# Gated linear attention into a cosine-gated MLP on one core: the first pair through the MLP as one unit of 256 tokens, pair 4 turned by DMA, 52 zero products for 54, and a new order of all steps

## The chip, the cores and the metric

The kernel runs on 1 core of one Trainium2 chip. The metric is the device time of one execution in microseconds (us). Three runs of the kernel before gave 182.62, 182.84 and 184.4 us; the median is 182.84 us.

## The reference

Two stages follow each other. The first is a gated linear attention over 4 batches, 8 heads, 768 positions and a head width of 48; the second is an MLP (the kernel's names call it MoE, though it has one expert) over the 3072 tokens that come out, with 384 inputs and 2048 hidden features.

```python
f = 1.0 / (1.0 + np.exp(-f_logit))                 # (4, 8, 768, 48)
for t in range(S):
    state = f[:, :, t, :, None] * state + np.einsum('bhd,bhe->bhde', k[:, :, t], v[:, :, t])
    y[:, :, t] = np.einsum('bhd,bhde->bhe', q[:, :, t], state)
x = y.transpose(0, 2, 1, 3).reshape(B * S, H * D)  # (3072, 384)
h = x @ w_in                                       # (3072, 2048)
g = h * np.cos(h)
out = g @ w_out                                    # (3072, 384)
```

All inputs and the output are float32 in DRAM; products are made in bf16.

## The kernel before

**Tiling.** The tokens are cut into 12 pairs of 256 tokens (two blocks of 128), three pairs to a batch. Within a pair the attention is done block-wise with matrix products, and a state (`sz`) is carried from block to block and from pair to pair. The MLP is done in units: `UNITS` cuts the 3072 tokens into two units of 128 tokens (both halves of pair 0) and then eleven of 256.

**Steps.** `describe` makes some 950 named steps with what each reads and writes. In a name the number is the pair (for the MLP the unit). Those that matter below are, in the order in which a pair passes through them:

- `f`, `k`, `q`, `v`: the loads, 384 KB each (192 KB for the halves `.0` and `.1` in pairs 0 and 1). `w0.i`, `w1.i`: the loads of the four quarters of `w_in` and of `w_out`, 768 KB each, into slots of the buffer `g`; `wc0.i`, `wc1.i`: their casts to bf16.
- `ex`, `ln`, `fx`, `fy` (ScalarE): exponentials and logarithms of the gate. `ad` (GpSimd) and `cum` (TensorE): their sums along the tokens. `eb`, `ei` (ScalarE): the decays. `qa`, `ka`, `qm`, `km` (GpSimd or VectorE): q and k with the decays in them.
- `tq`, `tk`: q and k turned. For pairs outside `TURN_QK` these are eight TensorE transposes for each half of the heads (line 435), with a copy `qkt` out of PSUM; for pairs in `TURN_QK` it is one DMA transpose for each half (line 424), issued from the SP queue.
- `sc` (line 456): scores, 8 products of 48x128 for each half where TensorE turned, 16 of 48x64 where the DMA did. `am` (VectorE): the mask. `ps` (line 479), `st`, `sz`: the state. `y`, `yi` (line 531): the pair's attention output, `xe`: its copy to `x`.
- `h` (line 579): x times `w_in`, 6 products for each step of a 256-token unit, 12 for each step of a 128-token unit. `co` (ScalarE, line 584): cosine. `g` (VectorE, line 561): h times its cosine. `o` (line 595): g times `w_out`, four products a step. `ot`, `out`: the copy and the store of 128 tokens.
- `zf`: a product of a zero tile with itself, 128x512, whose result nobody reads (line 264). `ZEROS` says how many there are.

**What sets the order.** `ORDER` is one long string. Each word names a step, the engine that does it (T TensorE, S ScalarE, V VectorE, G GpSimd, Y the SP queue) and, behind that, the buffer slots or PSUM banks that it takes. `emit` makes the instructions in the order of the words; each engine and each queue does its own instructions strictly in that order, and waits in front of an instruction until what it needs is there. SP issues nearly all loads, stores and DMA transposes from one queue.

```python
    for word in ORDER.split():
        name, how = word.split(":")
        plan.append((G.steps[name], LETTER[how[0]], [int(x) for x in how[1:].split(",") if x]))
    ...
        s.fn(e)
```

Of the kernel before, what the change touches and what calls it, by code (L numbers as in the profile page):

```python
# [15 lines left out]
B, H, S, D = 4, 8, 768, 48  # L16
# [11 lines left out]
TURN_QK = range(5, 12)  # L28
UNITS = [128, 128] + [256] * 11
# [3 lines left out]
ZEROS = 54  # L33
# [3 lines left out]
zvt.2:V zsp.1:V zsp.0:G zsz.3:V f0.1:Y0 f0.0:S zqk.0:G k0.0:Y0 ex0.1:S ex0.0:S k0.1:Y ln0.1:S1  # L37
zf0:T0 zf1:T0 zf2:T0 zf3:T0 zf4:T0 zf5:T0 zf6:T0 zf7:T0 zf8:T0 zf9:T0 cum0.1:T0 ln0.0:S cum0.0:T1
fx0.0:S ei0.1:S0 fx0.1:S ei0.0:S ka0.0:V f1.1:Y1 km0.0:G0 f1.0:Y ex1.1:S ka0.1:V zf10:T2 zf11:T2
zf12:T2 zf13:T2 zf14:T2 zf15:T2 zf16:T2 zf17:T2 tk0.0:T2 eb0.1:S0 ex1.0:S ln1.1:S1 ln1.0:S fx1.0:S  # L40
q0.1:Y0 q0.0:Y v0:Y0 fx1.1:S eb0.0:S qa0.1:V zqk.1:V qm0.1:V vb0:S0 f3:Y2 k1.1:Y1 km0.1:V qa0.0:V
zf18:T3 cum1.1:T3 zf19:T4 zf20:T4 zf21:T4 tq0.1:T0 cum1.0:T1 qm0.0:G zsz.2:G eb1.0:S1 vt0.3:S2
k1.0:Y ei1.0:S0 ex3:S zf22:T4 zf23:T4 zf24:T4 zf25:T4 zf26:T4 ps0.1:T4,5 ps0.0:T tk0.1:T v1:Y1 f2:Y0
qkt0.1:V0 eb1.1:S ln3:S0 ei1.1:S ka1.0:G q1.0:Y0 tq0.0:T ka1.1:G km1.1:G0 zvt.1:G vt0.0:S ad3:G1
vt0.1:G q1.1:Y vb1:S1 qkt0.0:V1 vt0.2:G zsz.1:G ex2:S w0.1:Y0 w0.0:Y1 k3:Y0 q3:Y1 w0.3:Y2 ln2:S1
vt1.2:S1 fy3:S zf27:T6 zf28:T6 zf29:T6 zf30:T6 zf31:T6 zf32:T6 sc0.0:T0 sz0.01:V2 sz0.00:V w0.2:Y3
ad2:G0 vt1.0:G km1.0:V vt1.3:G wc0.1:G am0.0:V0 zf33:T6 zf34:T6 yi0:T4 sc0.1:T2 am0.1:V1 st0.11:V
sz0.11:V3 wc0.0:G k2:Y1 zf35:T6 zf36:T6 zf37:T6 zf38:T6 ps1.1:T6,7 tk1.0:T0 ps1.0:T zf39:T1 zf40:T1
zf41:T1 cum3:T1 fy2:S ei3:S0 fx3:S ka3:G eb3:S2 vt1.1:S fx2:S km3.0:G1 qa3:G qm3.0:G km3.1:G qm3.1:G
w1.0:Y0 qa1.0:V st0.10:V qa1.1:V qm1.0:V wc0.2:G ka2:G q2:Y2 tk1.1:T2 zf42:T3 zf43:T3 y0:T3 tq1.0:T  # L50
xe0.1:S0 sz0.10:V st1.00:V st1.01:V qm1.1:V v2:Y1 zf44:T5 zf45:T5 zf46:T5 zf47:T5 zf48:T5 tq1.1:T
cum2:T1 sz1.00:V1 qkt1.0:V0 eb2:S0 xe0.0:S ei2:S1 qkt1.1:V1 km2.0:G0 km2.1:G zf49:T5 sc1.0:T4
sz1.01:V zf50:T0 zf51:T0 sc1.1:T2 h0.01:T0 st1.11:V sz1.11:V2 am1.1:V0 wc1.0:G qa2:G zf52:T6 zf53:T6
h0.00:T co0.0:S0 qm2.1:G am1.0:V1 h1.01:T2 h1.00:T co1.0:S1 y1:T6,4 yi1:T g0.0:V1 xe1.1:V1 st1.10:V
qm2.0:G vb2:G1 sz1.10:V g1.0:V4 w1.2:Y3 xe1.0:S tk3.0:T5 h2.01:T0 tq3.0:T w1.3:Y0 qkt3.0:V0 v3:Y0
f4:Y0 h2.10:T6 h2.00:T sc3.0:T4 tq3.1:T2 tk3.1:T h2.11:T wc1.2:G wc1.3:G vt2.1:G1 wc0.3:S vb3:G0
co2.0:S1 am3.0:V0 g2.0:V2 h2.20:T4 h2.21:T h0.11:T0 co2.1:S0 qkt3.1:S1 co2.2:S1 sc3.1:T2 w1.1:Y3
g2.1:V am3.1:V1 g2.2:V h0.10:T h1.11:T6 h1.10:T h2.30:T2 tk2.1:T4 tk2.0:T5 co0.1:S0 co1.1:S2 g0.1:V
g1.1:V h2.31:T o2.0:T0 co2.3:S0 tq2.1:T vt3.2:G2 vt3.1:G tq2.0:T o0.0:T1 o3.0:T6 o1.0:T7 qkt2.0:S2
vt2.0:S g2.3:V qkt2.1:V3 sc2.0:T2 ex4:S o3.2:T o0.2:T am2.0:V2 ln4:S1 ps2.0:T4 sc2.1:T2 vt2.3:G  # L60
ps2.1:T am2.1:V3 st2.01:V st2.00:V sz2.01:V1 sz2.00:V wc1.1:S f5:Y2 ex5:S ln5:S0 o1.2:T o2.3:T
o3.3:T o0.3:T o2.2:T q4:Y2 ps3.0:T4,5 ps3.1:T zsz.0:G vt2.2:G ad4:G0 yi2:T2,3 y2:T vt3.3:G sz3.01:V0
sz3.00:V o1.3:T cum4:T4 v4:Y0 vt3.0:G ad5:G0 fy4:S eb4:S0 st3.11:V fx4:S k4:Y1 fy5:S qa4:G qm4.0:G1
fx5:S ei4:S1 o0.1:T o2.1:T o3.1:T xe2.0:V1 st3.10:V sz3.10:V1 qm4.1:G sz3.11:V xe2.1:V ot2:V0
h3.00:T2 o1.1:T cum5:T0 ei5:S0 eb5:S2 k5:Y0 h3.01:T ot0:V1 vb4:G0 ka4:G y3:T4,5 yi3:T q5:Y1 h3.10:T0
h3.11:T co3.0:S0 xe3.0:V0 xe3.1:V ot1:V2 ot3:V3 co3.1:S2 g3.0:V4 h3.21:T4 h3.20:T co3.2:S1 h4.21:T6
h4.20:T g3.1:V ka5:G km4.0:G co4.2:S0 km4.1:G vt4.1:G2 qa5:G h4.11:T2 h4.10:T g3.2:V co4.1:S2
h4.31:T0 k6:Y2 qm5.1:G0 h4.30:T vt4.0:G vt4.2:G km5.1:G f6:Y1 v5:Y0 v6:Y1 f7:Y0 tq4.0:T4 tq4.1:T5
out3:Y tk4.0:T tk4.1:T co4.3:S1 g4.2:V2 h3.31:T6 h3.30:T qkt4.1:S0 qkt4.0:V1 g4.1:V o5.1:T4 co3.3:S0
o5.2:T o5.0:T o4.1:T5 g4.3:V g3.3:V ps4.1:T0,1 ps4.0:T st4.01:V st4.00:V sc4.1:T2 sc4.0:T6 am4.1:V0  # L70
am4.0:V1 sz4.00:V0 sz4.01:V qm5.0:G vt4.3:G st4.10:V tq5.1:Y2 sz4.10:V2 o5.3:T o4.2:T km5.0:G o4.0:T
o4.3:T ex6:S ln6:S0 vb6:G0 ad6:G0 ex7:S cum6:T2 y4:T3,6 tq5.0:Y3 yi4:T ot5:S3 st4.11:V sz4.11:V
vb5:G1 fx6:S ln7:S1 ei6:S0 eb6:S1 xe4.1:S1 o6.2:T4 out5:Y ad7:G0 ka6:G km6.0:G1 km6.1:G vt5.0:G2
vt5.1:G ps5.0:T2 ps5.1:T xe4.0:S st5.01:V sc5.0:T6 am5.0:V0 out0:Y k7:Y0 q6:Y1 q7:Y2 fy6:S fx7:S
f9:Y2 sc5.1:T0 cum7:T3 o6.3:T o6.1:T vt5.3:G h4.01:T6 h4.00:T st5.00:V am5.1:V1 sz5.01:V0 vt6.3:G1
qa6:G eb7:S0 ot4:S1 ka7:G ei7:S1 ps6.1:T3,5 ps6.0:T sz6.01:V1 sz5.00:V sz6.00:V v7:Y0 co4.0:S0
qm6.0:G h5.00:T0 h5.01:T co5.0:S1 vt5.2:S g4.0:V st6.11:V fy7:S h5.31:T2 h5.30:T o6.0:T y5:T6,7
yi5:T g5.0:V4 co5.3:S0 ot6:S3 tq6.0:Y0 xe5.1:S0 xe5.0:S f8:Y1 km7.0:G0 qa7:G km7.1:G qm7.1:G qm7.0:G
qm6.1:G h5.20:T0 h5.21:T st6.10:V sz6.10:V3 sz6.11:V g5.3:V tq7.1:Y2 tq6.1:Y3 vt6.2:S co5.2:S1
h5.10:T4 h6.20:T6 h6.21:T g5.2:V h5.11:T h6.10:T2 h6.11:T o7.2:T0 o8.2:T1 o7.0:T o8.3:T co6.2:S0  # L80
co5.1:S2 co6.1:S1 g6.2:V1 ex9:S g5.1:V out4:Y ln9:S1 sc6.0:T4 sc7.1:T6 g6.1:V am6.0:V0 ex8:S ln8:S0
fx8:S am7.1:V1 vt6.1:G vb7:G1 vt7.1:G2 vt6.0:S tq7.0:Y1 o7.3:T o7.1:T ps7.1:T4,5 ad9:G0 sc6.1:T2
ps7.0:T fx9:S ot7:V1 am6.1:V2 o8.1:T st7.00:V cum9:T6 o9.1:T0 o8.0:T sc7.0:T2 ad8:G1 cum8:T7
sz7.00:V0 am7.0:V3 q8:Y1 out6:Y o9.3:T o9.2:T ei9:S1 vt7.3:S fy9:S vt7.0:G eb8:S1 ei8:S0 fy8:S
eb9:S2 k8:Y0 out1:Y st7.01:V sz7.01:V v8:Y0 vt7.2:G qa8:G h6.01:T2 h6.00:T st7.10:V ot8:V3 sz7.10:V2
st7.11:V y6:T4,6 sz7.11:V xe6.0:S1 yi7:T1,7 yi6:T xe6.1:V y7:T o9.0:T xe7.1:V2 co6.0:S1 xe7.0:V
h7.31:T4 h6.31:T6 h6.30:T qm8.0:G0 ka8:G km8.0:G ot9:S2 v9:Y1 g6.0:V h8.21:T0 h7.30:T k9:Y2 vb8:G1
qm8.1:G co6.3:S2 vb9:G0 ka9:G tq8.0:Y0 q9:Y2 g6.3:V co7.3:S1 h8.20:T co8.2:S0 h7.20:T2 h7.21:T
h7.11:T6 co7.2:S2 h7.10:T g7.3:V4 h8.10:T4 out2:Y h8.11:T co7.1:S1 g8.2:V2 km8.1:G qa9:G f10:Y1
km9.0:G1 km9.1:G qm9.0:G co8.1:S0 g7.2:V h7.01:T0 h7.00:T o11.3:T2 o10.1:T3 g8.1:V k10:Y1 out8:Y  # L90
vt8.1:G2 f11:Y0 o11.1:T o10.3:T o12.3:T4 o10.2:T co7.0:S2 g7.0:V tq8.1:Y3 tq9.0:Y1 o12.0:T g7.1:V
ps8.1:T5 ex10:S ln10:S0 vt9.0:G1 ad10:G1 qm9.1:G ps9.1:T6,7 sc8.0:T0 ps9.0:T ps8.0:T am8.0:V1
o12.1:T o11.0:T cum10:T0 ex11:S fx10:S ln11:S1 ei10:S1 vt8.0:S eb10:S0 st8.00:V sz9.00:V1 st8.01:V
sz9.01:V st9.10:V sz8.01:V0 sz8.00:V o12.2:T o10.0:T st9.11:V o13.0:T6 ot10:S3 ot12:S0 o13.2:T
v10:Y1 ad11:G0 sz9.11:V3 sc9.0:T4 sc8.1:T0 cum11:T3 out12:Y o13.3:T o13.1:T o11.2:T am8.1:V3
am9.0:V0 sz9.10:V tq9.1:Y2 ka10:G vt8.3:G out10:Y km10.0:G0 vt8.2:G vt9.1:G km10.1:G ot11:V0 ei11:S0
eb11:S1 vt9.2:S vb10:S1 fx11:S yi8:T0,1 y8:T vt9.3:G xe8.0:S1 fy10:S q10:Y2 v11:Y0 out9:Y
ps10.0:T7,4 ps10.1:T sc9.1:T2 qa10:G k11:Y1 xe8.1:V qm10.0:G q11:Y1 am9.1:V1 st10.00:V st10.01:V
o14.1:T5 h8.01:T0 h8.00:T ot13:S3 co8.0:S1 sz10.01:V0 sz10.00:V st10.10:V o14.2:T h8.30:T2 h8.31:T
g8.0:V ka11:G h9.31:T6 h9.30:T co8.3:S2 tq10.0:Y0 o14.0:T y9:T0,1 yi9:T g8.3:V co9.3:S1 fy11:S  # L100
xe9.0:S2 o14.3:T qm10.1:G km11.1:G1 km11.0:G vb11:G0 zqk.2:G zsp.2:G h9.01:T2 h9.00:T co9.0:S2
ot14:S2 st10.11:V sz10.10:V1 g9.3:V1 out14:Y out11:Y sz10.11:V xe9.1:V h9.11:T6 h9.10:T co9.1:S1
h9.20:T0 h9.21:T g9.0:V g9.1:V h10.10:T4 tq10.1:Y1 co9.2:S2 out7:Y g9.2:V h10.00:T2 h10.11:T
h10.20:T6 vt11.3:S1 co10.1:S1 g10.1:V4 h10.01:T co10.0:S2 o16.1:T0 h10.21:T o16.0:T g10.0:V o16.2:T
o16.3:T sc10.0:T2 co10.2:S1 out13:Y ot16:S3 g10.2:V sc10.1:T4 ps11.1:T1 vt11.0:G vt10.3:G2 ps11.0:T
qa11:G vt11.1:S qm11.1:G st11.01:V tq11.1:Y2 sz11.01:V2 am10.0:V0 am10.1:V1 h10.31:T6 o17.3:T0
# [82 lines left out]
def describe(nc, cpool, ppool, q, k, v, f_logit, moe_w_in, moe_w_out, out):  # L189
# [420 lines left out]
    t0 = 0  # L610
    for m, T in enumerate(UNITS):
        moe(m, t0, T)
# [105 lines left out]
```

## Time and profile before

| what | value |
|---|---|
| time of the runs | 182.62, 182.84, 184.4 us (median 182.84) |
| span of the profiled execution | 180.9 us |
| median time less that span | 1.94 us |
| TensorE busy | 172.6 us (95%) |
| VectorE, ScalarE, GpSimd busy | 134.6, 130.7, 109.2 us |
| last TensorE product ends | about 177.6 us |
| moved by DMA | 33.93 MB, 188 GB/s in the mean |

The span goes from the first to the last instruction of the profiled execution. The times are of the whole execution as the device counts it; the profiled execution has no time of its own in the list beyond its span, so the 1.94 us are the median less the span. Two sorts of durations are used: a row of the timeline shows when a group starts and how long it is busy, with the latency of its last product; a piece of the chain shows how far a group moves the end, without that latency.

### The profile page before, as it was taken

The numbers are of one execution on the slowest core, as the hardware profiler recorded it, in microseconds if no ns is written. First come the engines' busy times: TensorE is split into PE (matmuls) and PEld (weight loads), VectorE is DVE, ScalarE is ACT, GpSimd is POOL, SyncE is SP. The second block draws the span as 40 slices with busy tenths as digits, with TensorE's granted clock in tenths as the row PEclk, the third lists the DMA queues.
The fourth block names the chain that finished last, engine by engine and source line by source line (L and its number), as shares of the span: only waits on it lengthen the run. The fifth ranks groups of instructions, "written<-read, shape, count | busy, mean of one in ns | idle before, by whom it ended". The sixth has DMA issues, their size and how long they took to land.

```text
span 180.9 us, 5814 instructions
## 1 busy us (share of the span) xinstructions
PE 172.6 (95%) x2460; PEld 123.9 (69%) x2464; DVE 134.6 (74%) x206; ACT 130.7 (72%) x187; POOL 109.2 (60%) x139
## 2 busy tenths in 40 slices
PE   7899789999999999999999999999999999999992
PEld 2455467785668977778667886658788767787651
DVE  5259988897595988897999697689888894356260
ACT  3985987777878899989997899769768452473221
POOL 4229899999969986989665977890798000000000
PEclk9999999999999999999999999999999999999999
DMA  5999999999999944986899999559927500110313
GB/s 149 261 261 276 343 320 341 250 318 284 301 265 233 274 83 123 252 210 145 122 180 308 173 267 278 124 131 251 203 92 182 100 4 0 43 47 4 130 43 131
DMA packets 72282, 33.93 MB, mean 188 GB/s; under 512 B 65344, under 2 KB 70720, under 8 KB 72256
## 3 DMA queue, kind: packets, MB, share of 16 engines
q1 hardware_dynamic: 71584, 33.27, 75.7%
q8 instruction: 19, 0.31, 0.7%
q10 hardware_dynamic: 672, 0.30, 0.6%
q14 instruction: 7, 0.06, 0.1%
HBM read 25.17 MB, written 4.72 MB: 165 GB/s over the span
## 4 chain that ended last, share of the span: by engine, by line
PE 81%; DMA 7%; ACT 3%; DVE 3%; SPq 2%; issue 1%; ACTq 0%
PE ps L595 35%; PE ps L579 33%; PE ps L531 5%; DMA f<-in_f_logit_dram 4%; PE ps L456 4%; DMA v<-in_v_dram 3%; SPq L296 2%; PE ps L479 2%; DVE g L561 1%; PE ps L435 1%; PE ps L374 1%; DVE am L461 1%; PE ps L264 1%; ACT f L344 0%; ACT f L329 0%
## 5 line engine op out<-in xcount | busy, mean ns | idle before, releaser
L561 DVE TENSOR_TENSOR g<-ps,co 128x1024 bf16<-128x1024 f32 x48 | 57.4, 1220 | 18.0 <-ACT co L584 16.7
L595 PE MATMUL ps<-w_out_bf,g 128*128 128x384 bf16 x384 | 68.9, 326 | 0.0
L579 PE MATMUL ps<-x,w_in_bf 128*128 128x256 bf16 (+1 forms) x624 | 68.1, 264 | 0.5 <-DVE x L197 0.4
L584 ACT ACTIVATE co<-ps,halfpi 128x1024 bf16<-128x1024 f32 x48 | 52.7, 1113 | 19.8 <-PE ps L579 19.5
L579 PEld LDWEIGHTS <-w_in_bf 128*128 128x128 bf16 x624 | 56.3, 98 | 9.2 <-DVE x L197 0.6
L595 PEld LDWEIGHTS <-g 128*128 128x128 bf16 x384 | 36.1, 98 | 21.4
L461 DVE TENSOR_TENSOR am<-ps,pmask 128x1024 bf16<-128x1024 f32 x24 | 28.7, 1218 | 5.2 <-PE ps L456 4.9
L404 POOL TENSOR_TENSOR qk<-k,bi 128x384 bf16<-128x384 f32 x22 | 22.0, 1008 | 5.4 <-ACT bi L391 4.7
L404 POOL TENSOR_TENSOR qk<-q,b 128x384 bf16<-128x384 f32 x21 | 20.8, 1000 | 2.7 <-DVE q L338 2.1
L197 POOL COPY vt<-vb 64x384 bf16<-64x384 bf16 x33 | 16.7, 507 | 1.6
L264 PE MATMUL ps<-zero 128*128 128x512 bf16 x50 | 14.6, 412 | 1.5 <-DVE zero L203 1.2
L503 DVE TENSOR_TENSOR sz<-ps,b 64x192 bf16<-64x192 f32 x40 | 14.1, 354 | 2.5 <-PE ps L479 1.6
L363 POOL TENSOR_TENSOR sp<-ls 128x384 bf16<-128x384 f32 x10 | 10.3, 1028 | 7.8 <-ACT ls L333 6.1
L341 POOL TENSOR_TENSOR q<-f,q 128x384 f32<-128x384 f32 x10 | 10.0, 998 | 8.0 <-DMA q<-in_q_dram 5.8
L329 ACT ACTIVATE f<-f 128x768 f32<-128x768 f32 (+1 forms) x14 | 10.4, 746 | 4.4 <-DMA f<-in_f_logit_dram 4.4
L497 DVE TENSOR_TENSOR ps<-ps,sz 64x192 f32<-64x192 f32 x32 | 11.7, 367 | 2.2 <-PE ps L479 1.1
L351 POOL TENSOR_TENSOR k<-k,f 128x384 f32<-128x384 f32 (+1 forms) x12 | 11.1, 931 | 3.4 <-DMA k<-in_k_dram 3.4
L197 ACT COPY ot<-ps 128x384 f32<-128x384 f32 (+1 forms) x14 | 6.1, 453 | 8.7 <-PE ps L595 8.7
L197 ACT CAST x<-ps 128x384 bf16<-128x384 f32 x12 | 5.5, 479 | 6.0 <-PE ps L531 6.0
L456 PE MATMUL ps<-qkt 48*64 48x128 bf16 (+1 forms) x304 | 8.7, 218 | 1.1 <-ACT x L197 0.8
L197 DVE CAST x<-ps 128x384 bf16<-128x384 f32 x12 | 6.4, 553 | 4.1 <-PE ps L531 3.9
L264 PEld LDWEIGHTS <-zero 128*128 128x128 bf16 x54 | 4.8, 103 | 5.9 <-issue 1.9
(64 smaller groups left out, 167.2 us busy)
## 6 DMA issues: line engine op xcount, KB each, us to landing
v<-in_v_dram SPq DMA_DIRECT2D x12, 384.0 KB, 5.9
out_dram<-ot SPq DMA_DIRECT2D x22, 192.0 KB, 2.3
f<-in_f_logit_dram SPq DMA_DIRECT2D x10, 384.0 KB, 6.0
k<-in_k_dram SPq DMA_DIRECT2D x10, 384.0 KB, 6.6
q<-in_q_dram SPq DMA_DIRECT2D x10, 384.0 KB, 6.7
g<-in_moe_w_in_dram SPq DMA_DIRECT2D x4, 768.0 KB, 7.5
g<-in_moe_w_out_dram SPq DMA_DIRECT2D x4, 768.0 KB, 6.1
k<-in_k_dram SPq DMA_DIRECT2D x4, 192.0 KB, 4.5
```

Source lines behind the costliest of these rows:

```text
L197: (nc.scalar.copy if e == "ACT" else eng(e).tensor_copy)(out=o, in_=i)
L264: G.step(f"zf{i}", ("PE",), lambda e, dump=dump: nc.tensor.matmul(dump.ap, lhsT=zero[:, 0:128], rhs=zero, start=True, stop=True), writes=[ ...
L351: eng(e).tensor_mul(out=w.ap[:, :, 0, :], in0=w.ap[:, :, 0, :], in1=t.ap[:, :, 0, :])
L404: G.step(f"{nm}{n}.{u}", ("POOL", "DVE") if cut else ("POOL",), lambda e, u=u, j=j, src=src, dec=dec: eng(e).tensor_mul(out=qkp[u][j].ap[: ...
L456: nc.tensor.matmul(o[t0:t1, r, 2 * a + g, :].rearrange("p (e n) -> p e n", e=2), lhsT=wide[s, t0 // 64, :] if turned else wide[s].rearrang ...
L461: G.step(f"am{n}.{u}", ("DVE",), lambda e, u=u, sc=sc: nc.vector.tensor_mul(out=am[u].ap.rearrange("p r b n -> p (r b) n"), in0=sc.ap.rear ...
L497: nc.vector.tensor_add(out=view()[s], in0=view()[s], in1=S0.ap[s, :, r, :])
L503: eng(e).tensor_mul(out=new.ap[s, :, r, :].rearrange("p (u a) n -> p u a n", u=2), in0=view()[s].rearrange("p (u a) n -> p u a n", u=2), i ...
L561: nc.vector.tensor_mul(out=o.rearrange("p b (n e) -> p b n e", e=2), in0=ph.ap.rearrange("p (b e n) -> p b n e", e=2, n=64), in1=co.ap.rea ...
L579: nc.tensor.matmul(ph.ap[:, i * T:(i + 1) * T].rearrange("p (g t) -> p g t", t=C), lhsT=w_in_bf[:, kk, f0:f0 + 128], rhs=xa[:, :, kk, :], ...
L584: G.step(f"co{m}.{j}", ("ACT",), lambda e, ph=ph, co=co: nc.scalar.activation(out=co.ap, in_=ph.ap, func=AF.Sin, bias=halfpi), reads=[ph], ...
L595: nc.tensor.matmul(po.ap[:, 0:DM], lhsT=gT.ap[:, j, i * C:(i + 1) * C], rhs=w_out_bf[:, j, :], start=(po.first and j == 4 * s), stop=(po.f ...
```

## The change

Only constants and the text of `ORDER` change; no function does. `TURN_QK` takes in pair 4, so that its four steps of TensorE transposes and its two copies out of PSUM are gone and two DMA transposes come in their place. `UNITS` makes both halves of pair 0 one unit, so that all unit numbers behind it fall by one and the two units of 128 tokens become one of 256. `ZEROS` goes from 54 to 52. All words of `ORDER` stand in new places with new slots.

```diff
-TURN_QK = range(5, 12)
-UNITS = [128, 128] + [256] * 11
+TURN_QK = range(4, 12)
+UNITS = [256] * 12
...
-ZEROS = 54
+ZEROS = 52
...
-zvt.2:V zsp.1:V zsp.0:G zsz.3:V f0.1:Y0 f0.0:S zqk.0:G k0.0:Y0 ex0.1:S ex0.0:S k0.1:Y ln0.1:S1
+zvt.2:V zsp.2:V f0.1:Y0 zqk.2:G zsp.0:G f0.0:S ex0.1:S ln0.1:S2 f1.0:Y2 ex0.0:S fx0.1:S ln0.0:S
...
```

By the words of `ORDER`, the zero products before the first product of the MLP are 52 of 54 before (the other two stand between that product's two halves), and all 52 in the changed order, the last four of them right ahead of it. Bytes asked for ahead of the first `w_in` quarter are the same in both, 3840 KB.

**ScalarE, from the load of the last early gate to the first cosine.** `f` and `ls` are the gate (`ex`, `ln`, `fx`, `fy`), `x` the copies `xe` of pair 0's output, `bi` and `b` the decays, `vt` the copies of v, `qkt` a copy of turned q and k, `co` a cosine. Before:

```order
L329 ACTIVATE f_94<-f_94 128x768
L333 ACTIVATE ls_110<-f_94 128x768
L197 COPY vt_124<-vb_121 64x8x48
L344 ACTIVATE f_96<-f_96 128x8x48
L344 ACTIVATE f_94<-f_94 128x8x48
L395 ACTIVATE bi_114<-ps_158 128x384
L347 ACTIVATE f_96<-ls_109 128x8x48
L395 ACTIVATE b_113<-ps_158 128x392
L197 COPY vt_124<-vb_121 64x8x48
L347 ACTIVATE f_94<-ls_110 128x8x48
L197 CAST x_139<-ps_160 128x384
```

In the changed kernel:

```order
L329 ACTIVATE f_94<-f_94 128x768
L333 ACTIVATE ls_109<-f_94 128x768
L347 ACTIVATE f_94<-ls_109 128x8x48
L197 CAST x_139<-ps_159 128x384
L197 COPY vt_123<-vb_121 64x8x48 x2
L344 ACTIVATE f_95<-f_95 128x8x48
L197 COPY qkt_128<-ps_160 128x1024
L347 ACTIVATE f_95<-ls_110 128x8x48
L395 ACTIVATE bi_115<-ps_158 128x384
L395 ACTIVATE b_112<-ps_158 128x392
L584 ACT_TABLE_LOAD
```

Eight instructions stood between the last early logarithm and the first copy of `x`; now one does, and the copy of turned q and k of pair 1 has come to ScalarE behind it.

**The SP queue around the first DMA transposes.** Before, the rows of `TURN_QK`'s first pair (pair 5) and the loads around them:

```order
L296 DMA k_99<-in_k_dram 128x8x96
L296 DMA f_95<-in_f_logit_dram 128x8x96
L296 DMA v_103<-in_v_dram 128x8x96
L296 DMA v_104<-in_v_dram 128x8x96
L296 DMA f_94<-in_f_logit_dram 128x8x96
L606 DMA out_dram<-ot_155 128x384
L424 DMA_TRANSPOSE qkt_128<-qk_117 128x8x128
L424 DMA_TRANSPOSE qkt_129<-qk_117 128x8x128
L606 DMA out_dram<-ot_155 128x384
```

In the changed kernel, where the first two transposes are pair 4's and the next two pair 5's:

```order
L296 DMA f_96<-in_f_logit_dram 128x8x96
L424 DMA_TRANSPOSE qkt_126<-qk_117 128x8x128
L424 DMA_TRANSPOSE qkt_127<-qk_117 128x8x128
L606 DMA out_dram<-ot_154 128x384
L424 DMA_TRANSPOSE qkt_128<-qk_119 128x8x128
L296 DMA f_94<-in_f_logit_dram 128x8x96
L424 DMA_TRANSPOSE qkt_129<-qk_119 128x8x128
L296 DMA k_99<-in_k_dram 128x8x96
L296 DMA v_105<-in_v_dram 128x8x96
L606 DMA out_dram<-ot_152 128x384
L296 DMA q_102<-in_q_dram 128x8x96
```

The load of k for pair 6 (the row `k_99` in both) stood ahead of all transposes; now it stands behind four of them, and v and q of pair 6 behind it.

**The end of ScalarE's list.** Before, both halves of the last output tile are copied there:

```order
L584 ACTIVATE co_148<-ps_160,halfpi 128x1024
L197 COPY ot_155<-ps_161 128x192 x2
L606 DMA out_dram<-ot_155 128x192
L713 UNCONDITIONAL_BRANCH
```

In the changed kernel one half is:

```order
L584 ACTIVATE co_151<-ps_161,halfpi 128x1024
L197 COPY ot_154<-ps_158 128x384
L197 COPY ot_155<-ps_158 128x384
L197 COPY ot_152<-ps_160 128x192
L606 DMA out_dram<-ot_152 128x192
L713 UNCONDITIONAL_BRANCH
```

The other half has gone to VectorE.

## Prediction before the run

> **What bounds the kernel now.** I read the page's busy times first, then the windows, then the chain, then TensorE's timeline where the windows show holes.
>
> ```profile
> span 180.9 us, 5814 instructions
> PE 172.6 (95%) x2460; PEld 123.9 (69%) x2464; DVE 134.6 (74%) x206; ACT 130.7 (72%) x187; POOL 109.2 (60%) x139
> PE 81%; DMA 7%; ACT 3%; DVE 3%; SPq 2%; issue 1%; ACTq 0%
> 20.00:25.00 5.00, 3.87 (x40) 2.05 (x42) 4.27 (x12) 4.95 (x12) 4.88 (x5) 1.00 1.13 320
> 25.00:30.00 5.00, 4.58 (x112) 3.94 (x110) 4.32 (x5) 4.00 (x5) 4.84 (x6) 1.00 1.04 337
> 35.00:40.00 5.00, 5.00 (x80) 4.62 (x77) 4.71 (x5) 4.10 (x4) 4.92 (x6) 1.00 0.94 264
> 170.00:175.00 5.00, 5.00 (x35) 3.18 (x34) 2.08 (x3) 1.11 (x1) 0.00 (x0) 1.00 0.00 0
> 171.58 6.01 PE L595 MATMUL ps<-w_out_bf,g 128*128 128x384 bf16 x36
> ```
>
> TensorE is busy 95% of the span and holds 81% of the chain. In a row of windows the first figure behind the length is TensorE's busy time, the last three are its granted clock, the DMA share and GB/s. From 35 us to the last product at 177.6 TensorE has no hole. So the time is a sum of three: the head, in which TensorE waits or multiplies zeros; the products that count; and a tail of 180.9 - 177.6 = 3.3 us. A change gains only by fewer or cheaper products, by a head that ends earlier, or by a shorter tail. What it takes from ScalarE, VectorE or GpSimd is worth nothing by itself.
>
> Where the head ends is the next question.
>
> ```profile
> 23.57 0.40 PE L456 MATMUL ps<-qkt 48*128 48x128 bf16 x8 [0.78 <-ACT x L197]
> 24.77 0.84 PE L579 MATMUL ps<-x,w_in_bf 128*128 128x128 bf16 x12
> 25.45 0.59 PE L264 MATMUL ps<-zero 128*128 128x512 bf16 x2
> 25.88 2.17 PE L579 MATMUL ps<-x,w_in_bf 128*128 128x128 bf16 x36
> 28.88 0.40 PE L435 MATMUL ps<-ident,qk 128*128 128x128 bf16 x4
> 29.70 0.83 PE L579 MATMUL ps<-x,w_in_bf 128*128 128x256 bf16 x6 [0.42 <-DVE x L197]
> 30.59 1.47 PE L579 MATMUL ps<-x,w_in_bf 128*128 128x256 bf16 x12
> 32.20 0.40 PE L456 MATMUL ps<-qkt 48*128 48x128 bf16 x8
> 32.99 3.07 PE L579 MATMUL ps<-x,w_in_bf 128*128 128x256 bf16 x30
> 35.99 0.40 PE L456 MATMUL ps<-qkt 48*128 48x128 bf16 x8
> ```
>
> The MLP begins at 24.77. By then the attention of pairs 0 and 1 is done but for pair 1's output, and both orders have the same products behind them there. From 24.77 on TensorE still loses time. I price it with the chain's pieces, which leave out latency:
>
> ```profile
> 26.05 0.68 PE ps L579 x12
> 75.88 1.31 PE ps L579 x12
> 54.12 0.65 PE ps L595 x4
> 63.08 0.89 PE ps L435 x16
> 43.34 0.33 PE ps L456 x8
> 89.78 0.57 PE ps L456 x32
> ```
>
> Twelve 128-token products take 0.68, twelve 256-token ones 1.31 (in the group of 30 there are 18 of 256 and 12 of 128: 1.96 + 0.68 = 2.64). The steps from one start to the next less the work are 25.88 - 25.45 = 0.43 (two zeros), 0.82 - 0.22 = 0.60, 1.61 - 1.31 = 0.30 and 3.00 - 2.64 = 0.36: 1.7 us lost before 36 us, of which the busy digits show only a part.
>
> **The change part by part.** *Units.* Pair 0 needed 96 products of 128 tokens, 8 x 0.68 = 5.44; it now needs 48 of 256, 4 x 1.31 = 5.24. That is 0.20 less, all on TensorE. The number of cosines and gate products (48 each) stays.
>
> *Pair 4 by DMA.* TensorE loses 16 transposes, 0.89. Its scores go from 16 products at 0.33 for eight (0.66) to 32 in 0.57, 0.09 less. Together 0.98, in the stretch without holes, so all of it counts. Two copies out of PSUM go too (one each on ScalarE and VectorE), which count for nothing while TensorE is the bound. What comes in:
>
> ```profile
> L424 SPq DMA_TRANSPOSE qkt<-qk x14: 1232/1248/2691, 65.1 to 140.0; - x14
> DMA to landing us min/median/max: 3.0/3.2/5.1
> k<-in_k_dram SPq DMA_DIRECT2D x10, 384.0 KB, 6.6
> ```
>
> Each transpose holds SP for 1.25 us (2.69 at most) and lands after 3.2 (5.1 at most). Its cover is the MLP of units 2 and 3: seven steps of 1.31, 9.2 us, and four of `o` stand on TensorE between `cum5` and pair 4's scores. I cost it at nothing; without that cover it would be the landing, up to 5.1. Behind them on SP stand two transposes of pair 5 and the loads of pair 6, which is a rival below.
>
> The DMA Engines page of the Trainium skill (DMA: Bandwidth & Descriptors, section on latency and other measured facts) gives 261 GB/s for such a transpose; the 256 KB of one would be an estimated 1.0 us by it. The 3.2 us to landing here speak for the longer price; by the page the sum would be the same and the rival on SP a little cheaper.
>
> *Zero products.* Two fewer are worth nothing as long as TensorE waits anyway. Their places count: the two inside the first MLP step go (0.43 of the 1.7). Four stand right ahead of the new first step; at the 0.43 for two above, that is 0.87 of delay if its operands are there already.
>
> *The start of the MLP.* I follow the new order on the engine that sets it, ScalarE.
>
> ```profile
> 17.71 0.84 ACT L329 ACTIVATE f<-f 128x768 f32<-128x768 f32 x1 [1.73 <-DMA f<-in_f_logit_dram]
> 18.58 0.84 ACT L333 ACTIVATE ls<-f 128x768 f32<-128x768 f32 x1
> 19.45 0.51 ACT L197 COPY vt<-vb 64x384 bf16<-64x384 bf16 x1
> 23.06 0.46 ACT L197 CAST x<-ps 128x384 bf16<-128x384 f32 x1
> 34.86 1.00 ACT L197 COPY qkt<-ps 128x1024 bf16<-128x1024 bf16 x1
> 22.18 2.87 POOL L197 CAST w_in_bf<-g 128x1536 bf16<-128x1536 f32 x2
> ```
>
> The gate load that ends at 17.7 has the same 3072 KB ahead of it in both orders, so I let it land at the same time. From there the new list is `ex3` 0.84, `ln3` 0.84, `fx3` 0.51, `xe0.0` 0.46 (20.4 us), two `vt` and `fy3` at 0.51 each (21.9), `qkt1.0` 1.00 (22.9). Then TensorE: `sc1.0` 0.33, four zeros 0.87: the first MLP step at 24.1. The other leg is the first quarter of `w_in`: same bytes ahead, GpSimd's sum `ad3` after `ln3`, one `vt`, a cast of 1.46, ready near 22.7, which does not decide. For the handing over between engines that I left out I add 0.15 and take 24.25: 0.5 earlier than 24.77. Bounds: 1.3 earlier if the zeros cost nothing, 1.0 later if what ScalarE waited for before (the decays behind `cum`, 0.8 in row 23.57) turns up at `qkt1.0`.
>
> *Loss behind it.* In the new order 5.2 us of pair 0's and 1's steps on the first two quarters, `y1` and then the next two quarters follow with hardly a hole: the third cast can be done at 28.3 and TensorE asks for it at about 30.4. I find 0.4 us by durations alone; the old order's 1.7 shows what handing over adds, so I take 1.0: 0.7 gained. Bounds 0.4 and 2.5.
>
> *Tail.* The two halves of the last tile's copy ran one behind the other on ScalarE; now VectorE does one.
>
> ```profile
> 177.63 0.54 ACT L197 COPY ot<-ps 128x192 f32<-128x192 f32 x2 [4.74 <-PE ps L595]
> ```
>
> 0.2 gained of the 0.54; bounds 0 and 0.3. (The last products are the same in kind.)
>
> *Every other step moved.* From 36 to 177.6 the old order has no hole, so a new one cannot gain there and can only lose. No row of before prices it. Below it is 0; above, the price of one late load, 4.3 (worked out below). The other engines have 26% or more of slack in the mean, and in the stretches that I followed, the transitions at pairs 2 to 5, each cosine and gate product comes 1 to 2 us before TensorE asks; that is nearer to the lower end, and I take 0.4.
>
> Sum: -0.20 - 0.98 - 0.5 - 0.7 - 0.2 + 0.4 = -2.2. The span goes from 180.9 to 178.7. Around it lie 182.84 - 180.9 = 1.94 us, so the time is **180.6 us**, 1.2% below the median of the runs.
>
> **The rivals.** *The head gives nothing.* The loads in the head run at 320 to 337 GB/s, the DMA share is above 1, and the weights are needed in any order; if each step merely waits elsewhere, start and loss stay as they were, and units, pair 4 and tail remain, 1.4, less the 0.4: 182.84 - 1.0 = 181.8. For it: ScalarE and GpSimd are busy 4.95 and 4.88 of 5 us in that window. Against it: two zeros and the 0.60 for `x` have no place in the new order.
>
> *The whole gain.* Handing over adds nothing, no new hole: start 0.8, loss 1.3, the rest 1.4, together 3.5: 179.3. For it: a stretch of 140 us without a hole shows that an order can be met to the last step. Against it: the head, where the old order wasn't.
>
> *A slower kernel: pair 6 late behind the transposes.* The place is SP's queue. Before, k of pair 6 was asked for before 50 us, ahead of every transpose; now it stands behind `tq5.0`, which waits for `km5.0`, the last of some twenty GpSimd steps behind the last weight cast. Its steps cost:
>
> ```profile
> L404 POOL TENSOR_TENSOR qk<-k,bi 128x384 bf16<-128x384 f32 x22 | 22.0, 1008 | 5.4 <-ACT bi L391 4.7
> L197 POOL COPY vt<-vb 64x384 bf16<-64x384 bf16 x33 | 16.7, 507 | 1.6
> GB/s 149 261 261 276 343 320 341 250 318 284 301 265 233 274 83 123 252 210 145 122 180 308 173 267 278 124 131 251 203 92 182 100 4 0 43 47 4 130 43 131
> ```
>
> The last quarter completes 12.2 MB of loads. The first ten of these slices, of 4.52 us each, move 12.7 MB, so it lands near 44.8, and its cast of 1.46 ends at 46.3. Thirteen steps of about 1.0, four `vt` and two `vb` of 0.8 are 17.7 us more: `km5.0` at 64, the request at 65.5, its landing, at the median 6.6, at 72. GpSimd is free at 70.6 and waits; `ka6`, two `km6` and `vb6`, 3.8 together, put pair 6's state products at 76. TensorE reaches them at 24.25 plus 17 steps of `h` (22.3), 27 of `o` (17.6), 11.2 of attention in pieces like those above and 1.0 of loss: 76.3. So there is 0.3 us of slack. With both transposes at their longest hold (1.4 more each) and the load 1.8 longer than its median, 4.6 later less 0.3 is a hole of 4.3 on TensorE: 180.6 + 4.3 = 184.9. It decides from a hole of 2.2 us on, where 182.84 is passed. For it: the hold of 2.69 is in the trace. Against it: all three have to come together.
>
> *A cold clock.* The row of the first ten zero products stands here because fewer zeros may let TensorE's rate fall:
>
> ```profile
> 1.19 3.69 PE L264 MATMUL ps<-zero 128*128 128x512 bf16 x10 [1.19 <-DVE zero L203]
> ```
>
> They take 0.37 each, while two at 25.45 move the next start by 0.43, 0.22 each: a start from rest costs 10 x 0.15 = 1.5. Were it to come twice, the time would be 182.1. The granted clock in the windows is 1.00 all along, and the longest hole that I find in the new head is 1.3 us, ahead of the first `cum`. The TensorE page of the Trainium skill (TensorE: Matmul & The Clock Gate, part 1) says that the clock halves after an idle window of about 3.4 us; the holes here stay far below, so by that rule it would not come.
>
> **How the numbers follow.** Likeliest is the sum, 180.6 (180.0 to 181.2), with 0.40. The head giving nothing, 181.8 and around to 182.8, has 0.26; the cold clock 0.04; the whole gain, 179.3, 0.17; the late pair 6, 184.9, 0.13. A measurement of this kernel tells about 1% from no change: 181.0 and 184.7 are the borders. Faster by over 1% is the whole gain, 0.17, and most of the likeliest case, 0.33: 0.50. Slower by over 1% is half of the late pair 6 and a little for places that I did not follow: 0.12. The rest is 0.38. The range is 178.6 to 184.9: it holds the bounds of start and loss on the good side and the late load on the other. The likeliest case's own range is 180.0 to 181.2.
>
> **What would show it.** Right: no 128-token product of `w_in` and 64 transposes on TensorE; the first MLP product near 24.2; under 1.2 us of loss in the 11 us behind it; TensorE without a hole from there to about 174.5 to 175.5; the last copies side by side on two engines. Wrong: a first MLP product after 24.8 (the start), rows of TensorE that wait for `wc` casts between 30 and 47 us (the loss), or a wait of over 1 us between 60 and 80 us with GpSimd idle on the load of k (the late pair).

## The result, and the profile after

| runs on one chip, alternating | before | changed | ratio (95%) | difference |
|---|---|---|---|---|
| first | 182.81 us (4 runs) | 181.1 us (180.52 to 181.87, 4 runs) | 0.9904 [0.9875, 0.9933] | -1.8 us |
| again, another chip | 183.03 us (29 runs) | 181.8 us (181.4 to 182.42, 6 runs) | 0.9941 [0.9922, 0.9959] | -1.1 us |

The difference is the ratio times the median of before. 180.6 us was forecast; the kernel is faster by 1.1 to 1.8 us, right at the 1% that the prediction took as the border of no change. The second measurement was expected at 0.990 of before like the first, and came out slower. The ratios here and below compare executions within 1.5% of their kernel's fastest, which leaves out, among others, four of twelve with four zeros less (184.2 us or more, the profiled one among them) and one of six with four words moved (200.3 us at a mean granted clock of 0.854).

The page of the changed kernel, its first lines and the shares of its chain:

```profile
span 179.3 us, 5727 instructions
PE 171.0 (95%) x2412; PEld 122.9 (69%) x2414; DVE 137.8 (77%) x206; ACT 131.3 (73%) x185; POOL 109.2 (61%) x139
PE 69%; DMA 10%; POOL 7%; SPq 5%; DVE 5%; issue 3%; ACT 0%; POOLq 0%; DVEq 0%; ACTq 0%
```

TensorE is still busy for 95% of the span, yet its part of the chain fell from 81% to 69%: DMA, GpSimd and SP's queue now hold 22% of what set the end, where they held 9% (DMA and SP's queue) before. These shares do not repeat: in the second profile of the same kernel TensorE has 40%, and in the kernel of the tail experiment below, which differs from it only at the very end, 80%. So they say that other engines now come close to TensorE, and not by how much; the holes below say that.

Windows of the changed kernel (length, TensorE busy, its weight loads, VectorE, ScalarE, GpSimd, granted clock, DMA share, GB/s):

```profile
20.00:25.00 5.00, 4.39 (x56) 2.39 (x46) 4.86 (x9) 4.30 (x9) 5.00 (x6) 1.00 1.04 326
25.00:30.00 5.00, 5.00 (x95) 4.28 (x94) 4.07 (x8) 4.02 (x5) 4.64 (x4) 1.00 0.99 306
70.00:80.00 10.00, 9.45 (x223) 7.46 (x221) 8.59 (x16) 8.71 (x14) 8.49 (x11) 1.00 1.22 282
110.00:120.00 10.00, 9.36 (x166) 5.93 (x164) 6.55 (x11) 8.36 (x16) 5.42 (x7) 1.00 0.80 195
```

From 25 to 30 us TensorE is now full (4.58 of 5 us before). In exchange there are holes in two later stretches, where the old order had none. The timeline of TensorE (start, us, line, tile, count, idle time before and what ended it) shows them:

```profile
23.04 0.40 PE L456 MATMUL ps<-qkt 48*128 48x128 bf16 x8 [0.45 <-DVE qkt L197]
24.05 1.04 PE L264 MATMUL ps<-zero 128*128 128x512 bf16 x4
24.92 1.47 PE L579 MATMUL ps<-x,w_in_bf 128*128 128x256 bf16 x12
27.22 9.34 PE L579 MATMUL ps<-x,w_in_bf 128*128 128x256 bf16 x84
...
77.19 0.50 PE L579 MATMUL ps<-x,w_in_bf 128*128 128x256 bf16 x3
78.07 3.11 PE L579 MATMUL ps<-x,w_in_bf 128*128 128x256 bf16 x27 [0.38 <-issue]
...
111.72 0.42 PE L456 MATMUL ps<-qkt 48*64 48x128 bf16 x16 [0.64 <-DMA qkt<-qk]
```

The MLP starts at 24.92 (24.77 before), then 84 products run without a hole. At 111.7 us TensorE waits for a DMA transpose, which is the second one of pair 8.

**Where the time went.** For a balance of all runs I take, from one TensorE instruction's start to the next, what lies above the step of its kind (0.109 us for a 256-token product of `w_in`, 0.163 for one of `w_out`, 0.216 for a zero product, and so on), and call it loss. Zero products count as work in it. The single old-order kernels in the table are those of the experiments below.

| us | first MLP product | loss in the 11.2 us behind it | from there to 70 | 70 to 100 | 100 to 120 | behind 120 |
|---|---|---|---|---|---|---|
| before | 24.77 | 1.35 | 0.80 | 1.00 | 0.27 | 0.57 |
| old order with all three constants of the change | 24.87 | 1.46 | 1.00 | 0.90 | 0.26 | 0.57 |
| changed | 24.92 | 0.11 | 0.75 | 1.40 | 1.09 | 0.52 |
| changed, again | 24.98 | 0.11 | 1.05 | 1.12 | 1.42 | 0.52 |
| changed, four words of the order moved | 25.12 | 0.11 | 0.74 | 1.63 | 0.27 | 0.52 |

The new order saves 1.35 us early and pays 0.2 to 0.5 between 70 and 100 and 0.8 to 1.2 between 100 and 120.

### The profile page after: what moved, and what is told of

The parts are those of the page before. It is cut to its first block, busy times and chain, and to the rows that moved or that the text cites. A ratio compares the mean times of both kernels' runs of the same rounds, so it can differ in the third digit from the quotient of the medians.

```text
span 179.3 us, 5727 instructions
## 1 busy us (share of the span) xinstructions
PE 171.0 (95%) x2412; PEld 122.9 (69%) x2414; DVE 137.8 (77%) x206; ACT 131.3 (73%) x185; POOL 109.2 (61%) x139
## 4 chain that ended last, share of the span: by engine, by line
PE 69%; DMA 10%; POOL 7%; SPq 5%; DVE 5%; issue 3%; ACT 0%; POOLq 0%; DVEq 0%; ACTq 0%
PE ps L595 29%; PE ps L579 29%; DMA q<-in_q_dram 7%; SPq L296 5%; PE ps L531 4%; DMA qkt<-qk 3%; PE ps L456 3%; POOL qk L404 3%; PE ps L479 1%; POOL sp L363 1%; PE ps L435 1%; DVE qk L404 1%; POOL vt L197 1%; DVE sz L503 1%; PE ps L374 1%
## 5 line engine op out<-in xcount | busy, mean ns | idle before, releaser
L579 PE MATMUL ps<-x,w_in_bf 128*128 128x256 bf16 x576 | 66.7, 273 | 0.4 <-issue 0.4
L584 ACT ACTIVATE co<-ps,halfpi 128x1024 bf16<-128x1024 f32 x48 | 52.6, 1115 | 17.7 <-PE ps L579 14.4
L404 POOL TENSOR_TENSOR qk<-q,b 128x384 bf16<-128x384 f32 x22 | 21.9, 1002 | 2.6 <-DVE q L338 1.7
L197 POOL COPY vt<-vb 64x384 bf16<-64x384 bf16 x31 | 15.9, 514 | 1.4
L351 POOL TENSOR_TENSOR k<-k,f 128x384 f32<-128x384 f32 (+1 forms) x13 | 11.7, 904 | 6.2 <-DMA k<-in_k_dram 2.9
L197 DVE COPY ot<-ps 128x384 f32<-128x384 f32 (+1 forms) x17 | 8.7, 519 | 8.5 <-PE ps L595 6.0
L197 ACT COPY ot<-ps 128x384 f32<-128x384 f32 (+1 forms) x9 | 4.1, 455 | 8.9 <-PE ps L595 8.9
```

Of the source, the lines that this page charges most:

```text
L197: (nc.scalar.copy if e == "ACT" else eng(e).tensor_copy)(out=o, in_=i)
L351: eng(e).tensor_mul(out=w.ap[:, :, 0, :], in0=w.ap[:, :, 0, :], in1=t.ap[:, :, 0, :])
L404: G.step(f"{nm}{n}.{u}", ("POOL", "DVE") if cut else ("POOL",), lambda e, u=u, j=j, src=src, dec=dec: eng(e).tensor_mul(out=qkp[u][j].ap[: ...
L579: nc.tensor.matmul(ph.ap[:, i * T:(i + 1) * T].rearrange("p (g t) -> p g t", t=C), lhsT=w_in_bf[:, kk, f0:f0 + 128], rhs=xa[:, :, kk, :], ...
L584: G.step(f"co{m}.{j}", ("ACT",), lambda e, ph=ph, co=co: nc.scalar.activation(out=co.ap, in_=ph.ap, func=AF.Sin, bias=halfpi), reads=[ph], ...
```

## The experiments

The theory that I went in with: pair 4's turning and the one unit bring what their products cost; the new order brings its gain right behind the start of the MLP and gives it back on the SP queue and the loads behind it. The rival: the order brings at least 0.3 us of its own.

### Parts of the change in the old order

**Pair 4 by DMA alone.**

```diff
-TURN_QK = range(5, 12)
+TURN_QK = range(4, 12)
-... tq4.0:T4 tq4.1:T5 out3:Y tk4.0:T tk4.1:T ... qkt4.1:S0 qkt4.0:V1 ...
+... tq4.1:Y0 tq4.0:Y1 out3:Y ...
```

> The old order with one part of the change alone: pair 4 turned by two DMA transposes, asked for on SP in the place where TensorE's transposes stood in the list, still behind the loads of pair 6. If the 0.98 us of TensorE's products is all that counts, the last product ends 1.0 earlier than 177.6 and the time falls by 0.9 to 1.1. If the SP queue pays for it (two holds of 1.25 us ahead of pair 7's loads and the stores), half or all of it comes back as holes on TensorE behind 75 us: a fall of 0 to 0.5.

Measured: 182.03 us for 182.95, ratio 0.9941 [0.9924, 0.9958], that is -1.08 us. The two transposes come and cost TensorE nothing that the time shows; the 0.98 of the prediction is met within the interval.

**One unit of 256 tokens alone**, all unit numbers behind it one less.

```diff
-UNITS = [128, 128] + [256] * 11
+UNITS = [256] * 12
-... h0.01:T0 ... h0.00:T co0.0:S0 ... h1.01:T2 h1.00:T co1.0:S1 ...
+... h0.11:T0 ... h0.10:T co0.1:S0 ... h0.01:T2 h0.00:T co0.0:S1 ...
```

> The old order with another part alone: pair 0 as one unit of 256 tokens, each of its steps in the place of the old step that used the same PSUM bank. If a unit is worth only its products, the time falls by 0.2 and the 1.7 us that TensorE lost between 24.8 and 36 us stay. If it is the larger unit that keeps TensorE busy there, the holes at 29 to 30 and 33 to 36 us close as well and the time falls by 0.9 to 1.5.

Measured: 182.59 us, ratio 0.998 [0.9972, 0.9989], -0.36 us. The holes behind the start stayed (loss 1.42 in those 11.2 us), so they are the order's and not the units'.

**Both together.** The two edits above in one kernel.

> The order of before, with two edits of the change and nothing else: pair 0 as one unit of 256 tokens, and pair 4 turned by DMA; 54 zero products as before. Theory: these two carry the whole gain, and the new order of all steps carries none (what it wins behind the start of the MLP it loses again in later holes). Then this is as fast as the changed kernel: ratio to before 0.991 to 0.994, -1.1 to -1.6 us, which is the sum of the two single edits (-0.36 and -1.08). Rival: the new order is worth 0.3 us or more of its own; then this stays at 0.9945 or above (-1.0 us or less). Second rival: the two edits share a cover (both take TensorE work away ahead of the same later wait), and together give clearly less than their sum: 0.995 or above, with a hole of TensorE of over 0.5 us that neither had alone.

Measured: 181.68 us for 182.93, ratio 0.9926 [0.9912, 0.9941], -1.35 us: the two edits add up, and the old order with them stands between the two measurements of the changed kernel.

**All three constants.** As before, and without the two zero products inside the first MLP step:

```diff
-ZEROS = 54
+ZEROS = 52
-... wc1.0:G qa2:G zf52:T6 zf53:T6 h0.10:T co0.1:S0 ...
+... wc1.0:G qa2:G h0.10:T co0.1:S0 ...
```

> The order of before with both edits (pair 0 as one unit, pair 4 by DMA) and without the two zero products that stand between the two halves of the MLP's first step; 52 zero products, as in the changed kernel. With this all three changed constants stand in the old order, and the new order of steps is the only difference left. Theory: the two zeros (0.43 us) lie on the path (second half, cosine, VectorE's product, the copy of x for which TensorE waits 0.45 us near 29.8 us), so all of it moves up: 0.3 to 0.5 us below the kernel with 54, ratio 0.989 to 0.992, as fast as the changed kernel or faster. Rival: TensorE's wait near 29.8 us takes the 0.43 us up (it would be 0.9 us then): ratio 0.9915 to 0.994, and the zeros were free. Second rival: with less work early the granted clock falls behind 26 us.

Measured: 181.33 us (181.15 to 182.05) for 182.91, ratio 0.9918 [0.9898, 0.9938], -1.50 us. Its page and the rows of TensorE behind the start (this kernel's line numbers are one lower, since `ORDER` fills one line less):

```profile
span 179.4 us, 5720 instructions
PE 81%; DMA 7%; ACT 3%; DVE 3%; SPq 2%; issue 1%; ACTq 0%
24.87 2.93 PE L578 MATMUL ps<-x,w_in_bf 128*128 128x256 bf16 x24
28.63 0.40 PE L434 MATMUL ps<-ident,qk 128*128 128x128 bf16 x4
29.37 0.82 PE L578 MATMUL ps<-x,w_in_bf 128*128 128x256 bf16 x6 [0.35 <-ACT x L196]
```

The wait for `x` comes at 29.37 where it came at 29.83 with 54 zeros: the whole 0.43 us moved up in the trace (TensorE's last product starts 0.47 earlier). The span is 179.4 us, against 179.3 and 179.7 of the changed kernel. So the old order with the three constants is as fast as the changed kernel, as far as a ratio of ±0.2% tells; the nearly one thousand words of the order that were placed anew bring nothing that can be measured. With these intervals up to about half a us either way stays possible.

### What the new order pays: pair 8 and SP's queue

The chain of the changed kernel between 90 and 112 us (start, us, what held the end; some pieces left out):

```profile
90.35 0.58 SPq L296
90.98 1.97 SPq L296
92.99 1.17 SPq L296
94.20 7.79 DMA q<-in_q_dram
...
104.05 1.00 POOL k L351
...
105.76 5.91 DMA qkt<-qk
111.72 0.42 PE ps L456 x16
```

Not TensorE but SP's queue, two transfers and GpSimd between them hold the end for 21 us: the load of q for pair 9 is asked for behind two loads of v and one of k, lands 7.79 us after its request, and GpSimd waits for it with pair 8's `qm8.0` behind it in its list; so pair 8's second transpose goes out at 105.76 and lands when TensorE has been waiting. The rows of SP and of GpSimd:

```profile
97.73 4.37 SPq L424 DMA_TRANSPOSE qkt<-qk  x1
105.76 2.85 SPq L424 DMA_TRANSPOSE qkt<-qk  x1
102.13 1.00 POOL L341 TENSOR_TENSOR q<-f,q 128x384 f32<-128x384 f32 x1 [4.53 <-DMA q<-in_q_dram]
```

**A first mend.** Two words moved: `qm8.0` ahead of `qa9` on GpSimd, `tq8.0` right behind `qm8.0`.

```diff
-... vt7.3:G qa9:G qm8.0:G vt7.1:S tq8.0:Y1 ...
+... vt7.3:G qm8.0:G tq8.0:Y1 qa9:G vt7.1:S ...
```

> The changed kernel with two steps of pair 8 moved: the product of q with its decay goes ahead of pair 9's step that waits for a load on GpSimd, and the DMA transpose of it goes on SP ahead of the loads of k, f and q for pairs 10 and 11. If SP's order made the hole of 0.6 us ahead of pair 8's second scores at 111.7 us (0.84 us lost with what is hidden), the hole is gone and the last product ends 0.6 to 0.9 earlier. If the hole only stood for a later bound, TensorE gets a hole of the same size between 112 and 135 us and the time stays within 0.2.

Measured: 181.84 us, ratio 0.9937 [0.9915, 0.996], as the unchanged one beside it (0.9941). A half-miss by my own placing: three loads still stood ahead of the transpose on SP, and it was issued at 105.06. The hole came to 0.25 us idle, and the loss between 100 and 120 us to 0.75.

**The whole mend.** Four words, `q9`, `qm8.0`, `tq8.0` and `f10` (the expectation counts five):

```diff
-... tq7.0:Y0 ... v9:Y0 v8:Y2 k9:Y2 q9:Y1 ...
+... tq7.0:Y0 q9:Y1 ... v9:Y0 v8:Y2 k9:Y2 ...
-... km8.1:G tq8.1:Y2 f11:Y2 ... q10:Y2 ... f10:Y1 vt7.3:G qa9:G qm8.0:G vt7.1:S tq8.0:Y1 ...
+... km8.1:G qm8.0:G tq8.1:Y2 tq8.0:Y1 f10:Y1 f11:Y2 ... q10:Y2 ... vt7.3:G qa9:G vt7.1:S ...
```

> The changed kernel with five words moved: on SP the load of q9 goes ahead of those of v9, v8 and k9, and the second transpose of pair 8 right behind the first, ahead of the loads of pairs 10 and 11; on GpSimd qm8.0 goes ahead of qa9. Theory: the hole of TensorE near 111.7 us (0.8 to 1.2 us lost) comes from SP's order here (q9 late by queueing, qm8.0 and the transpose behind it). Then GpSimd's wait of 4.5 us for q9 shrinks to under 3, the second transpose is issued at 102 to 103 instead of 105.8, the hole is under 0.25 us, and TensorE's last product ends 0.5 to 1.0 us earlier: ratio 0.987 to 0.991. Rival: the hole is slack of a later limit (pair 9 or 10's transposes and loads on the same queue); then the time stays at 0.992 to 0.995 and as much is lost behind 112 us instead.

SP, GpSimd and TensorE of this kernel:

```profile
90.84 0.58 SPq L296 DMA_DIRECT2D q<-in_q_dram  x1
98.84 5.18 SPq L424 DMA_TRANSPOSE qkt<-qk  x2
102.48 1.00 POOL L351 TENSOR_TENSOR k<-k,f 128x384 f32<-128x384 f32 x1 [1.07 <-DMA k<-in_k_dram]
111.35 0.40 PE L456 MATMUL ps<-qkt 48*64 48x128 bf16 x14
111.67 4.08 PE L595 MATMUL ps<-w_out_bf,g 128*128 128x384 bf16 x24
```

The hole is gone: both transposes leave SP by 104.0, GpSimd no longer waits for pair 9's q (4.53 us before; left between 92 and 112 us are 2.29 for pair 8's q and 1.07 for pair 9's k), and the loss between 100 and 120 is 0.27, that of the old order. The place and its cause, the order on SP and GpSimd here, are shown by this. The time is 181.41 us, ratio 0.9905 [0.9879, 0.993]: inside what the theory said, but also what the unchanged kernel gave on the first chip. In the profile TensorE ends 0.4 to 0.8 us earlier than in the two profiles of the changed kernel; in the medians that isn't settled.

### The zero products right ahead of the MLP

**Four zeros less.** `zf48` to `zf51` left out of the changed kernel, `ZEROS = 48`.

> The changed kernel without the four zero products that stand right ahead of the first product of the MLP. They take 0.87 us there and x and the first cast were ready at about 23.5 us. If they delay the MLP, its first product starts at 24.05 in place of 24.92 and the time falls by 0.6 to 0.9. If the steps behind it wait for something else (the casts of the weights, the copies of pair 1's x), the start moves and the gain is lost again as holes before 50 us: a fall of 0 to 0.2.

Measured: ratio 0.9949 [0.9922, 0.9977], median of all runs 182.76 us (180.78 to 184.54): not faster. The profiled execution took 184.53 us. Pair 8's second transpose on SP, TensorE's last product ahead of the hole, the hole and the windows behind it:

```profile
107.57 2.89 SPq L424 DMA_TRANSPOSE qkt<-qk  x1
111.53 0.28 PE L479 MATMUL ps<-vb,qk 64*64 64x48 bf16 x8
113.49 0.42 PE L456 MATMUL ps<-qkt 48*64 48x128 bf16 x16 [1.68 <-DMA qkt<-qk]
113.84 5.75 PE L595 MATMUL ps<-w_out_bf,g 128*128 128x384 bf16 x24
112.00:114.00 2.00, 0.51 (x17) 0.37 (x18) 1.90 (x4) 1.95 (x4) 0.84 (x1) 1.00 1.00 278
114.00:116.00 2.00, 2.00 (x9) 1.04 (x8) 1.64 (x3) 1.96 (x4) 1.86 (x4) 0.62 1.28 259
116.00:118.00 2.00, 2.00 (x8) 0.94 (x7) 0.56 (x1) 0.64 (x2) 1.51 (x2) 0.52 0.81 260
```

The MLP did not start earlier in this execution: its first product stood at 24.93, against 24.92 with the four zeros, because a load of q came late (next section). TensorE reached pair 8 later by 0.74 us (111.53, against 110.79), but the transpose went out later by 1.81 (107.57, against 105.76), so the wait is 1.68 us instead of 0.64. And behind the hole the granted clock falls to 0.62 and 0.52, so that 24 products take 5.75 us instead of 4.08 (the same group in the kernel with the four moves). This is the cold clock of the prediction's fourth rival, not at the start, where it was looked for, but 90 us later. That the hole brought it down is not shown: holes of 0.64, 0.98 and 1.17 us at the same place, in three other executions of this order, were followed by a clock of 1.00, and an execution of the old order with pair 4 by DMA (185.06 us, of which there is no trace) has the same mean granted clock, 0.99.

**Four zeros less and the four moves.**

> The same five moves, and the four zero products right ahead of the MLP left out too (48 in all). Theory: without these zeros the first product of the MLP starts 0.8 us earlier, and what ate that (the hole near 111.8 us, which grew to 1.7 us when only the zeros were left out, with the clock of TensorE down to 0.5 to 0.6 behind it) is gone: 0.8 us below the kernel with the five moves alone, no stretch with a granted clock under 0.95 behind 30 us. Rival: TensorE now runs into the DMA side somewhere else (pairs 9 to 11), and the time is within 0.3 us of the kernel with the moves alone. If the clock falls without a hole of over 1 us ahead of it, the hole did not cause it.

```profile
23.97 1.48 PE L578 MATMUL ps<-x,w_in_bf 128*128 128x256 bf16 x12
114.00:116.00 2.00, 2.00 (x18) 1.22 (x16) 1.33 (x2) 1.98 (x5) 1.97 (x3) 1.00 1.18 282
116.00:118.00 2.00, 2.00 (x38) 1.23 (x40) 1.11 (x2) 1.54 (x5) 0.74 (x1) 1.00 0.22 68
```

With the hole gone the clock stays at 1.00, which fits a fall brought by the hole, in one execution each. The MLP starts at 23.97, the earliest of all, 1.15 us before the kernel with the moves alone (0.87 of it the four zeros), but TensorE's last product starts only 0.5 us before; the loss from the first 11 us to 70 us grew by 0.54 (1.28 for 0.74). By the times, 181.35 us and 0.9906 [0.9874, 0.9938], it can't be told from it: the rival holds for the time. This and the kernel with the four moves have the lowest ratios apart from the first measurement of the change itself; none is shown to beat it.

### Why the MLP does not start earlier

On VectorE and GpSimd of the changed kernel, just ahead of the MLP:

```profile
16.76 1.15 DVE L351 TENSOR_TENSOR k<-k,f 128x192 f32<-128x192 f32 x1
16.53 1.17 POOL L404 TENSOR_TENSOR qk<-k,bi 128x384 bf16<-128x384 f32 x1
19.66 1.17 DVE L404 TENSOR_TENSOR qk<-q,b 128x384 bf16<-128x384 f32 x1
19.36 1.05 POOL L404 TENSOR_TENSOR qk<-q,b 128x384 bf16<-128x384 f32 x1 [1.67 <-DVE q L338]
22.31 0.67 DVE L197 COPY qkt<-ps 128x1024 bf16<-128x1024 bf16 x1
```

`qm1.1` on VectorE takes 1.17 us while GpSimd does `qm1.0` beside it; the product of k and its gate takes 1.15 beside another. Both end a few tenths behind GpSimd's. The copy `qkt1.1` that follows them ends at 22.98, and TensorE's scores at 23.04 wait for it. Behind these stand `cum3`, the other half of the scores at 23.72 and the four zeros at 24.05.

**`qm1.0` moved to VectorE**, so that the two no longer stand side by side:

```diff
-... qm1.1:V ... sz1.00:V qm1.0:G ...
+... qm1.1:V qm1.0:V ... sz1.00:V ...
```

> The changed kernel with one product of q and its decay (pair 1, first half of the heads) on VectorE, right behind the one for the second half, in place of GpSimd. In the changed kernel the one on VectorE took 1.17 us while GpSimd did the other, 0.50 to 0.56 where GpSimd was idle. If the two engines hold each other up, both now take about 0.55, together less than the 1.17 for one, VectorE is no later, GpSimd's sum and first cast come 0.5 to 1.0 earlier, and the time falls by 0 to 0.2 (the start of the MLP hangs on VectorE). If the 1.17 has its cause in the instruction itself, the second takes as long, the MLP starts 1.0 later and the time rises by 0.8 to 1.2.

```profile
16.38 0.34 DVE L351 TENSOR_TENSOR k<-k,f 128x192 f32<-128x192 f32 x1
16.39 1.19 POOL L404 TENSOR_TENSOR qk<-k,bi 128x384 bf16<-128x384 f32 x1
19.88 2.13 DVE L404 TENSOR_TENSOR qk<-q,b 128x384 bf16<-128x384 f32 x2
19.83 1.00 POOL L363 TENSOR_TENSOR sp<-ls 128x384 bf16<-128x384 f32 x1 [2.25 <-ACT ls L333]
```

Measured: 182.25 us, ratio 0.9967 [0.9948, 0.9987], 0.45 us slower than the changed kernel beside it. GpSimd filled the place with `ad3`, and the first of the two VectorE steps stood behind that. The same product of k that took 1.15 when it started behind GpSimd's took 0.34 here, where it started 0.01 us ahead of it, and GpSimd's took 1.19. The unchanged kernel's second profile has it too: there the product of k started 0.08 us ahead of GpSimd's and took 0.34. Nothing is won by that, for VectorE's next product then takes 1.24 and 1.25 us in these two profiles, where it took 0.56. So the pairing is shown by rows that differ in who came first, and the remedy failed: the MLP started at 26.11, a part of which is the late load below. The SBUF — State Buffer page of the Trainium skill (section on the two separate sides) says that a VectorE operation with two inputs in SBUF and a GpSimd operation that reads SBUF exclude each other for a whole instruction; 0.34 against 1.15 agrees.

The first MLP product of kernels with this same head lay at 24.92, 24.98, 25.12, 25.53, 25.62 and 25.75 us, and of the five kernels with the old head at 24.77 to 25.02. The new head is not earlier, and it is looser. In the three that lay at 25.5 or behind it VectorE had waited for the second load of q, and the product that uses it, begun behind one of GpSimd's, took 0.94 to 0.97 us where it took 0.35 in the changed kernel. The row of the kernel at 25.75:

```profile
19.45 0.94 DVE L338 SCALAR_TENSOR_TENSOR q<-f,q 128x192 f32<-128x192 f32 x1 [0.36 <-DMA q<-in_q_dram]
```

The profiled execution with four zeros less has the same row (0.94 behind a wait of 0.36), and so its MLP started no earlier.

### The tail

**Two buffers for the halves of the last tile**, so that the two copies cannot wait for each other by the buffer:

```diff
+                ot = ot if c0 == 0 or r0 // C < 23 else Val(otS)
-ot23.0:V
+ot23.0:V1
```

> The changed kernel with the two halves of the last output tile in two buffers of their own. In the changed kernel VectorE's half began only when ScalarE's had ended (176.40 after 176.05 plus 0.32). If the shared buffer orders them, both begin at 176.05 now and span and time fall by 0.3 to 0.4. If the order comes from the PSUM bank that both read, nothing moves.

The last copies of the changed kernel, then of this one:

```profile
176.05 0.32 ACT L197 COPY ot<-ps 128x192 f32<-128x192 f32 x1 [4.07 <-PE ps L595]
176.40 0.36 DVE L197 COPY ot<-ps 128x192 f32<-128x192 f32 x1 [2.27 <-ACT ot L197]
```

```profile
177.35 0.32 ACT L197 COPY ot<-ps 128x192 f32<-128x192 f32 x1 [4.07 <-PE ps L595]
177.71 0.36 DVE L197 COPY ot<-ps 128x192 f32<-128x192 f32 x1 [2.27 <-ACT ot L197]
```

Measured: 181.97 us, ratio 0.996 [0.9935, 0.9984]. VectorE still starts 0.04 us after ScalarE has ended, with no buffer in common any more. What both still share is the PSUM bank that they read. The PSUM — Partial Sum Buffer page of the Trainium skill (section on bank collisions) says that two engines may not read one bank in the same partitions at once, and that the back end puts a dependency between them; the two rows agree, though a kernel with two banks was not run.

### Undoing pair 4 in the changed kernel

```diff
-TURN_QK = range(4, 12)
+TURN_QK = range(5, 12)
-... tq4.1:Y0 tq4.0:Y1 ...
+... tq4.1:T0 tk4.1:T qkt4.1:S0 tq4.0:T1 tk4.0:T qkt4.0:V1 o5.0:T4 ...
```

> The changed kernel with pair 4 turned by TensorE again, sixteen transposes ahead of the first products of units 4 and 5's second half, and its copies on ScalarE and VectorE. If TensorE's products are what counts: 0.9 to 1.1 slower than the changed kernel, that is 182.0 to 182.2, with the holes at 77.7 and 111.7 us where they were (1 us later). If the transposes on SP made those holes by holding the loads up, they shrink by up to 1.2 us together and the time stays at 180.9 to 181.4.

Measured: 182.93 us, ratio 0.9997 [0.9967, 1.0027]. This one is not a clean price:

```profile
64.22 1.05 PE L435 MATMUL ps<-ident,qk 128*128 128x128 bf16 x16 [1.17 <-DVE g L561]
```

The transposes took PSUM banks that VectorE had not yet read, and waited 1.17 us, by my placing. The holes at 77 and 111 us were gone (loss between 100 and 120 us 0.42), and TensorE ended only 1.2 us later than in the profile of the changed kernel's second run (176.42 us), though by 70 us it lay 2.5 us behind it (0.64 at the first MLP product, 0.88 more loss from there, and pair 4's 0.98 of products). That fits holes that are set by the SP queue and not by TensorE; the price of pair 4 rests on the run in the old order.

## Why the prediction was right, and where not

The total came out 0.5 us above the forecast on the first chip and near the rival "the head gives nothing" (181.8) on the second. Term by term, by the rows and runs above:

| term | forecast | measured | from |
|---|---|---|---|
| units | -0.20 | -0.36 [-0.20, -0.51] | the edit alone |
| pair 4 by DMA | -0.98 | -1.08 [-0.77, -1.39] | the edit alone |
| start of the MLP | -0.5 | +0.15 | 24.77 to 24.92 |
| loss behind it | -0.7 | -1.6 | 1.7 to 0.11, the two zeros' 0.43 in it |
| tail | -0.2 | 0 | 3.3 us in both |
| every other step | +0.4 | +1.1 | loss from 36 us on, the last four columns: 2.64 to 3.76 (4.11 in the second profile) |

*Units and pair 4* held: products priced by their rows, on an engine without holes around them, add up one to one, alone and together (-0.36 and -1.08; -1.35 together).

*The start* is the term that failed by its mechanism. ScalarE's list was followed rightly: 22.9 us was forecast for the end of its `qkt1.0`, and it ended at 22.74. But the other leg that I looked at was the weights', and the one that decided was VectorE's, which I did not follow: two of its steps stood for over 1.1 us beside GpSimd's, and the last copy ended at 22.98. Nor did I count what TensorE then had to do ahead of `sc1.0`: `sc1.1` and `cum3`, 0.68 us, from 23.04 to 23.72. So `sc1.0` began 0.82 us behind the 22.9 of the working, which had 0.15 for this. The four zeros then cost 0.87 in full, as worked out. The sign named for a wrong start, a first MLP product after 24.8, came.

*The loss behind it* was mis-sized: durations gave 0.4, I took 1.0 because handing over had added to the old order, and 0.11 was measured. The upper bound of the gain (1.3) was passed. The old order lost its time to named waits, and where the new one has none of them, nothing is added.

*Every other step* was mis-sized the other way: 0.4 for the price of a place that I could not see, and 1.1 measured. The mechanism was in the text as the rival of pair 6: loads behind DMA transposes on SP, GpSimd idle for a load, the transpose late, TensorE waiting. Pair 6 itself was in time, its state products at 76.83 without a wait. The working for it had added GpSimd's steps up wrongly: 13 of 1.01 us, four of 0.51 and two of 0.8 make 16.7, not 17.7, which leaves 1.3 us of slack for 0.3. I followed pairs 2 to 6 and stopped; it came true at pair 8 with 0.8 to 1.2 us, not 4.3. The hole ahead of 78.07 us, inside one MLP step, came and went between two runs of the same kernel. Such a hole, of 0.16 to 0.68 us and marked issue, stands between 78 and 80 us in six of the nine profiles of the new order and in none of the five of the old; its cause is open.

*The tail* gave nothing, since the step took "side by side on two engines" for granted.

Not one of the errors is large; the total was near partly by luck, because a start, a late loss and a tail that were too good by 0.65, 0.7 and 0.2 us met an early loss that was too bad by 0.9. And the question that I did not ask is whether the order was needed at all: with the three constants the old order reaches the same time, within what the runs can tell.

## What to carry to other kernels

Price a change of constants and a change of order apart, and run the constants in the old order first: here they carry all of the gain that the runs can tell. A hole that is closed early in a stream that is bound elsewhere comes back at the next place where a queue or a transfer is late, so follow each queue to the end of the program and not only past the place of the edit. When one execution comes out far slower, look at the granted clock behind its longest hole: one late transfer was followed here by 24 products that took 5.75 us for 4.08.

## What the runs showed of the hardware

- In one execution the granted clock fell to 0.62 and 0.52 in two windows of 2 us after a hole of 1.68 us, with 0.51 us of TensorE work in the 2 us window in which it lay. The TensorE page of the Trainium skill (TensorE: Matmul & The Clock Gate, part 1) gives an idle window of about 3.4 us, and the prediction set its last rival aside by that; this hole was half as long. Holes of 0.64 to 1.17 us in three other executions were followed by 1.00.
- A VectorE product of two SBUF tiles that took 0.34 us when it started first took 1.15 when a GpSimd product had started 0.23 us ahead of it.
- A DMA transpose held SP for 4.37 us and another 2.85, where the longest hold before was 2.69; the second landed 5.91 us after its start, for a median of 3.2 before. What stood behind the first on the queue went out when its hold ended, at 102.20.
- Two engines that copy two halves of one PSUM tile went one behind the other, with 0.04 us between them.
